# Attention scores in two 64-row halves of the matmul array, with a 0/1 mask factor after the exp, in a block-sparse attention and MLP kernel

## The chip, the cores and the metric

The kernel runs on one core of one Trainium2 chip. The metric is device time in microseconds of one execution; the median over three runs of the kernel before is 324.76 us (324.6 to 324.99).

## What is computed

Batch 4, 8 heads, 768 positions, head size 64. The mask is built from 24 blocks of 32 positions: neighbours, the first and the last block, and three sampled blocks for each block of queries.

```python
scores = (q @ k^T) / sqrt(64)                # for each batch and head, 768 x 768
scores = where(mask, scores, -1e9)
attn   = softmax(scores)
x      = (attn @ v), heads side by side      # 4 x 768 x 512

a1  = alpha1 * x + beta1
tok = w_tok @ a1                             # over the 768 positions
u   = x + lam * tok
a2  = alpha2 * u + beta2
out = u + lam * (relu(a2 @ w_ch1) @ w_ch2)   # 512 -> 2048 -> 512
```

## The kernel before

**Units.** Two heads of one batch make a pair; there are 16 pairs, four for each batch, pair i belonging to batch i // 4. A pair has 12 units (i, c, j): c is one of two halves of 384 queries, j says which head of the pair (j // 3) and which two of its six key tiles of 128 (j % 3). A step s of the main loop (L735) works on one unit and on what else is due then.

**A step's order on TensorE.** `emit_qk` (L310) makes the scores of the step's unit: two matmuls of 88 rows (L324), one for each key tile, with 384 query columns, into two banks of one `sp` tile. 64 of the rows are the head size; the other 24 carry the mask: rows 64 to 87 of `kTs` hold, for each key, a value of 0 or -400 for each block of queries, and the same rows of `qTs` hold which block a query is in. A masked score so becomes -400 lower, and the exp (L332, ScalarE) gives 0 for it. Then comes poured work: `pour` (L650 on) takes matmul jobs of the MLP from a queue by credit (L553 the first product, L572 the second, L485 the mixing of positions, `job_tok`). Last comes `emit_pv` (L337) for the unit of two steps ago (`LAG = 2`): six matmuls (L345) that take the exp's output `eT` as weights and `vext` (v with a column of ones) as 65 moving columns. `emit_finish` (L354) divides by the sum, and `emit_a1pp` (L369) makes a1, on GpSimd but for a batch's last half.

**How q and k get there.** `emit_load` (L105) loads q, k and v of a pair from HBM on GpSimd's queue, with a cast to 16 bits, into `qr`, `kr`, `vr` with two buffers each. For pairs 1 to 5, `emit_lay` (L116) copies q and k side by side into `qk` on VectorE, and `emit_tps` (L264) transposes on TensorE, 12 transposes of 128 x 128 for a pair, from where VectorE copies into `kTs` (L273) and `qTs` (L276). From pair 6 (`XP = 6`), `emit_lay` copies q and k into `ql` and `kl`, padded to 128 columns for each tile and with the mask's columns put there once (`emit_mask_cols`, L281, six transposes of 24 rows at L285; `emit_mask_spread`, L290, on GpSimd), and `emit_tdma` (L298) issues one DMA transpose for q and one for k on SP's queue, 12 tiles each, at the fourth and fifth step of the pair before.

**Order.** The schedule is written out by hand: `slots` (L667 to L725) says at which step each piece of the first batch is emitted; the engines take their instructions in the order of emission. PSUM has two `sp` tiles, three `mm` tiles (poured work, transposes, other small products) and one `op` tile; `eT` has five buffers. SP's queue carries the DMA transposes of q and k, those of `uraw` (`emit_udma`) and the output. After the last unit the rest of the MLP of the last batch runs alone.

Of the kernel before, what the change touches and what calls it, by code (L numbers as in the profile page):

```python
# [11 lines left out]
FP = mybir.dt.float32  # L12
F16 = mybir.dt.float16
BF = mybir.dt.bfloat16
I32 = mybir.dt.int32
AF = mybir.ActivationFunctionType
ALU = mybir.AluOpType
# [3 lines left out]
S = 768  # L21
D = 64
BLK = 32
NBLK = S // BLK
NR = 3
DM = 512
P = 128
NT = S // P
NH = 4 * DM // P
QC = 384  # L30
NP = H // 2
XP = 6
BIG8 = 400.0
SCALE = 1.0 / 8.0
EXPB = -0.35667494
# [6 lines left out]
def kernel(  # L42
# [16 lines left out]
    nc = tc.nc  # L59
# [3 lines left out]
    indq_np = (tok[None, :] // BLK == np.arange(NBLK)[:, None]).astype(  # L63
        ml_dtypes.bfloat16
    )
# [9 lines left out]
    ms_np = np.concatenate([mstat_np] + [kbi_np] * NR, axis=1)  # L75

    ident_dr = nc.inline_tensor(np.eye(P, dtype=ml_dtypes.bfloat16), name="ident_c")
    indt_np = np.ascontiguousarray(
        indq_np.reshape(NBLK, NT, P).transpose(2, 1, 0).reshape(P, NT * NBLK)
    )  # L80
    indt_dr = nc.inline_tensor(indt_np, name="indt_c")
    indq_dr = nc.inline_tensor(indq_np, name="indq_c")
    ident8_dr = nc.inline_tensor(np.eye(8, dtype=np.float32), name="ident8_c")
    ms_dr = nc.inline_tensor(ms_np, name="ms_c")
# [4 lines left out]
    ap_ = ctx.enter_context(tc.tile_pool(name="attn", bufs=1))  # L89
# [4 lines left out]
    def ptile(shape, dt, name):  # L94
        return pp.tile(shape, dt, name=name, tag=name)
# [6 lines left out]
    raws = {}  # L102
    qks = {}

    def emit_load(i, which="qkv"):  # L105
        b, hp = i // NP, i % NP
        for nm, src, dt in (("q", q, BF), ("k", k, BF), ("v", v, F16)):
            if nm not in which or (i, nm) in raws:
                continue
            t = ap_.tile([P, 2, NT * D], dt, name=nm + "r", tag=nm + "r", bufs=2)  # L110
            nc.gpsimd.dma_start(  # L111
                t[:], src[b, 2 * hp : 2 * hp + 2].rearrange("w (p o) d -> p w (o d)", o=NT)
            )
            raws[(i, nm)] = t

    def emit_lay(i, nm, w=slice(0, 2), copy=None):  # L116
        raw = raws[(i, nm)][:, w].rearrange("p w (o d) -> p w o d", d=D)
        if nm != "v" and i >= XP:
            dst = (qls if nm == "q" else kls)[i % 2][:, w, :, 0:D]
        elif nm == "v":  # L120
            dst = vexts[i % NVB][:, w, :, 0:D]
        else:
            if i not in qks:
                qks[i] = ap_.tile([P, 2, NT, 2, D], BF, name="qk", tag="qk", bufs=2)
            dst = qks[i][:, w, :, "qk".index(nm), :]
        (copy or nc.vector.tensor_copy)(out=dst, in_=raw)  # L126


    for nm in "qkv":
        raws[(0, nm)] = ap_.tile(  # L130
            [P, 2, NT * D], FP, name=nm + "f", tag="otf_" + nm, bufs=1
        )
    sampi = ptile([P, 2 * NR], I32, "sampi")
    ms = ptile([P, (1 + NR) * NBLK], FP, "ms")
    identb = ptile([P, P], BF, "identb")
    NQB = 4
    qTs = [ptile([P, 2, S], BF, f"qTs{i}") for i in range(NQB // 2)]
    kTs = [ptile([P, 2, S], BF, f"kTs{i}") for i in range(NQB // 2)]
    qText = [qTs[n // 2][:, n % 2] for n in range(NQB)]
    kText = [kTs[n // 2][:, n % 2] for n in range(NQB)]  # L140

    qls = [ptile([P, 2, NT, P], BF, f"ql{i}") for i in range(2)]
    kls = [ptile([P, 2, NT, P], BF, f"kl{i}") for i in range(2)]
    indt = ptile([P, NT, NBLK], BF, "indt")
    maskt = ptile([P, NT, NBLK], BF, "maskt")

    def load_first(nm, src, w, eng):
        eng.dma_start(
# [26 lines left out]
        )  # L175
    for i in range(2, NQB):
        nc.sync.dma_start(qText[i][D : D + NBLK, :], indq_dr.ap())
    nc.sync.dma_start(indt[:], indt_dr.ap().rearrange("p (o n) -> p o n", o=NT))
    warm = ptile([P, DM], BF, "warm")
    nc.vector.memset(warm[:], 0.0)  # L180
    for t in vexts:
        nc.gpsimd.memset(t[:, :, :, D : D + 1], 1.0)
    for t in qls + kls:
        nc.gpsimd.memset(t[:, :, :, D + NBLK : P], 0.0)

    gate = ptile([P, 1], FP, "gate")
    nc.gpsimd.tensor_copy(out=gate[:], in_=raws[(0, "v")][:, 0, 0:1])
# [60 lines left out]
    def mm_tile(shape=(P, DM), dt=FP):  # L248
        return psum.tile(list(shape), dt, name="mm", tag="mm", bufs=3)
# [28 lines left out]
            )  # L278
            qa = qb

    def emit_mask_cols():  # L281
        tps = mm_tile((P, NT, NBLK), BF)
        rows = slice(D, D + NBLK)
        for o in range(NT):
            nc.tensor.transpose(  # L285
                tps[:, o, :], kText[0][rows, ts(o, P)], identb[rows, rows]
            )
        nc.vector.tensor_copy(out=maskt[:], in_=tps[:])

    def emit_mask_spread():  # L290
        for ts_, src in ((qls, indt), (kls, maskt)):
            for t in ts_:
                nc.gpsimd.tensor_copy(
                    out=t[:, :, :, D : D + NBLK],
                    in_=src[:].unsqueeze(1).broadcast_to([P, 2, NT, NBLK]),
                )

    def emit_tdma(i, nm):  # L298
        dst, src = ((qTs, qls) if nm == "q" else (kTs, kls))
        nc.sync.dma_start_transpose(  # L300
            out=dst[i % 2][:].rearrange("p w (o t) -> p (w o) t", t=P),
            in_=src[i % 2][:].rearrange("p w o d -> p (w o d)"),
        )

    ets = {}
    ops = {}
# [3 lines left out]
    def emit_qk(i, c, j, spare=0):  # L310
        w, jp = j // 3, j % 3
        n = (2 * i + w) % NQB
        sp = sp_tile()
        for jj in range(2):
            for _ in range(spare if jj else 0):
                nc.tensor.matmul(
                    sp[:, 0, QC:],
                    warm[:, 0:P],
                    warm[:, 0:P],
                    start=False,  # L320
                    stop=True,
                    skip_group_check=True,
                )
            nc.tensor.matmul(  # L324
                sp[:, jj, 0:QC],
                kText[n][0 : D + NBLK, ts(2 * jp + jj, P)],
                qText[n][0 : D + NBLK, ts(c, QC)],
                start=True,
                stop=True,
            )  # L330
        eT = ap_.tile([P, 2, QC], F16, name="eT", tag="eT", bufs=5)
        nc.scalar.activation(  # L332
            eT[:], sp[:, :, 0:QC], AF.Exp, bias=expb[:], scale=SCALE
        )
        ets[(i, c, j)] = eT

    def emit_pv(i, c, j):  # L337
        w, jp = j // 3, j % 3
# [330 lines left out]
    def at(s, *fns):  # L669
        slots.setdefault(s, []).extend(fns)  # L670
# [15 lines left out]
    at(6, lambda: emit_bcast(0))  # L686
    at(7, lambda: emit_bcast(1))
    at(8, lambda: emit_bcast(2))
    at(13, emit_mask_cols)
    at(14, emit_columns_use)  # L690
    at(60, emit_lam16)
    at(57, emit_mask_spread)
    for i, where in {
        1: (5, 7, 11, 9, 12),
        2: (16, 17, 18, 21, 23),
        3: (20, 21, 28, 27, 32),
        4: (34, 35, 40, 37, 39),
        5: (41, 42, 45, 47, 51),
    }.items():
        for n, nm in enumerate("qkv"):  # L700
            at(where[n], lambda i=i, nm=nm: emit_lay(i, nm))
        for w in range(2):
            at(where[3 + w], lambda i=i, w=w: emit_tps(i, w))
    for i, nm, s in ((3, "qk", 9), (3, "v", 12), (4, "qkv", 22), (5, "qkv", 33)):
        at(s, lambda i=i, nm=nm: emit_load(i, nm))
    for o in range(NT):
# [25 lines left out]
        for fn in slots.get(s, ()):  # L732
            fn()

    for s in range(len(units) + LAG + 1):  # L735
        if s < len(units):
            i, c, j = units[s]
            r = s % 12
            emit_qk(i, c, j, zeros.get(s, 0))
            if r == 2 and i + 2 < NPAIR:  # L740
                emit_load(i + 2)
            if XP <= i + 1 < NPAIR:
                if r in (3, 4):
                    emit_lay(i + 1, "qk"[r - 3])
                    emit_tdma(i + 1, "qk"[r - 3])
                if r == 6:
                    emit_lay(i + 1, "v")
        if s >= OPEN:
            fns(s)
        if s in ready:  # L750
            i = ready.pop(s)
            tok, _ = pair_jobs(i)
            queue[0:2] = tok + [(0.0, lambda i=i: emit_udma(i))] + queue[0:2]
            scales[s + 7] = i
        if s in scales:
            emit_uscale(scales.pop(s))
        if s >= OPEN:
            pour()
        if LAG <= s < len(units) + LAG:


            i, c, j = units[s - LAG]
            if j == 1:
                emit_pv(i, c, 0)
            if j > 0:
                emit_pv(i, c, j)
            if j == NT - 1:
                emit_finish(i, c)
                last = (i % NP, c) == (NP - 1, 1)
                emit_a1pp(i, c, nc.vector if last else nc.gpsimd)  # L770
                if last:
                    phase["first"] = False
                    queue.extend(mlp_jobs(i // NP))
                    left = per_b if i >= NP else 2 * per_b - OPEN
                    state["rate"] = (sum(t[0] for t in queue) + 6.2 - CARRY) / left
                elif c == 1 and i >= NP:
                    ready[s + 5] = i
        if s < OPEN:
            fns(s)
# [33 lines left out]
```

## Time and profile before

| what | value | where |
|---|---|---|
| median of three runs | 324.76 us (324.6 to 324.99) | times |
| the profiled execution, first to last instruction | 323.1 us | page |
| first and last score matmul (L324) | 6.2 and 259.5 us | line L324 |
| mean granted TensorE clock | 1.000 | cores |
| L332 exp, ScalarE | 192 x 901 ns | part 5 |
| L324 scores, TensorE | 384 x 326 ns | part 5 |
| L553 and L572, TensorE | 512 x 325 ns, 368 x 379 ns | part 5 |
| L345, TensorE | 1152 with 65 columns, 193 ns each | part 5 |
| kl and ql copies, VectorE | 10 x 826 ns, 10 x 378 ns | part 5 by shape |
| L376 and L377, GpSimd | 28 x 1009 ns, 28 x 952 ns | part 5 |
| DMA transposes issued on SP (q, k, u) | 10, 10, 11 | part 6 by queue |

The span is the time from the first to the last instruction of the one profiled execution; no other time of that execution is recorded, and the median of the runs lies 1.66 us above it. A matmul's duration in the profile is a model with much overlap: two matmuls that start 0.163 us apart are both shown with 0.326. What TensorE spends on one is read from the starts. A row such as "24*128 24x24" gives the rows and columns of the array that a matmul uses, then the shape of what moves.

### The profile page before, as it was taken

Reading aid. Unit: us, or ns where it says so; the run is one execution under the profiler, and the core shown is the slowest. Engines: PE = TensorE matmul, PEld = TensorE weight load, DVE = VectorE, ACT = ScalarE, POOL = GpSimd, SP = SyncE. Lnnn points to the kernel's source line nnn. Section 1 sums busy time; section 2 is a strip of 40 time slices with the busy share of each in tenths; the row PEclk is TensorE's granted clock in tenths of the full one; section 3 lists DMA queues with packets and bytes.
Section 4 is the critical chain, followed back from the end, with each engine's and each line's share of the span. In section 5 each row is a group of like instructions: output and inputs, shape, how many; then the busy total and the mean of one; then the engine's idle time right before and its main releaser. Section 6 shows DMA issues by size and latency. Waiting matters only on the chain.

```text
span 323.1 us, 7663 instructions
## 1 busy us (share of the span) xinstructions
PE 315.6 (98%) x3216; PEld 205.7 (64%) x3216; DVE 140.0 (43%) x289; ACT 223.2 (69%) x328; POOL 99.0 (31%) x128
## 2 busy tenths in 40 slices
PE   8889999999999999999999999999999999999996
PEld 3667878667675766676665756676665756555543
DVE  4889988557343345331534444242332434000011
ACT  4889998998878776878768675678877740553310
POOL 7566746443434411132525402142222200000000
PEclk9999999999999999999999999999999999999999
DMA  6999996969392976091665966097430011000012
GB/s 168 197 191 164 143 156 110 165 114 140 57 177 54 169 120 131 32 172 27 127 103 96 138 106 128 34 155 74 108 52 32 15 46 65 32 34 32 32 43 89
DMA packets 61898, 32.56 MB, mean 101 GB/s; under 512 B 42000, under 2 KB 58756, under 8 KB 61736
## 3 DMA queue, kind: packets, MB, share of 16 engines
q0 software_dynamic: 16608, 14.22, 31.2%
q1 hardware_dynamic: 44680, 17.23, 25.2%
q10 hardware_dynamic: 576, 0.62, 0.7%
q8 instruction: 25, 0.41, 0.5%
q14 instruction: 9, 0.07, 0.1%
HBM read 29.97 MB, written 6.29 MB: 112 GB/s over the span
## 4 chain that ended last, share of the span: by engine, by line
PE 90%; DVE 7%; POOL 1%; issue 1%; ACT 1%; DVEq 0%; POOLq 0%
PE mm L553 26%; PE mm L572 25%; PE sp L324 16%; PE mm L485 10%; PE op L345 9%; PE op L260 1%; PE mm L592 1%; DVE qTs L276 1%; DVE wtokT L469 1%; DVE kTs L273 1%; PE mm L267 1%; DVE qk L126 1%; DVE x_sb L362 1%; POOL a1pp L376 1%; POOL a1pp L377 1%
## 5 line engine op out<-in xcount | busy, mean ns | idle before, releaser
L332 ACT ACTIVATE eT<-sp,expb 128x768 f16<-128x768 f32 x192 | 170.4, 901 | 47.3 <-PE sp L324 44.6
L553 PE MATMUL mm<-uT,w1b 128*128 128x384 bf16 x512 | 100.1, 325 | 0.0
L324 PE MATMUL sp<-qTs,kTs 88*128 88x384 bf16 x384 | 95.5, 326 | 0.9 <-ACT eT L332 0.5
L572 PE MATMUL mm<-w2b,hts 128*128 128x512 bf16 x368 | 92.3, 379 | 0.0
L560 ACT ACTIVATE hts<-mm 128x384 bf16<-128x384 f32 x128 | 61.8, 488 | 35.4 <-PE mm L553 35.0
L376 POOL TENSOR_TENSOR a1pp<-x_sb,vbc 128x384 bf16<-128x384 f32 x28 | 28.3, 1009 | 150.7 <-DVE x_sb L362 150.7
L553 PEld LDWEIGHTS <-w1b 128*128 128x128 bf16 x512 | 49.3, 97 | 36.1 <-issue 0.9
L345 PEld LDWEIGHTS <-eT 128*128 128x128 f16 x1152 | 55.9, 97 | 21.9
L572 PEld LDWEIGHTS <-hts 128*128 128x128 bf16 x368 | 35.3, 97 | 33.9
L345 PE MATMUL op<-vext,eT 128*128 128x65 f16 x1008 | 53.8, 193 | 0.0
L581 DVE TENSOR_TENSOR ot<-x_sb,mm 128x512 f32<-128x512 f32 x23 | 15.8, 686 | 66.9 <-PE mm L572 66.9
L485 PE MATMUL mm<-a1pp,wtokT 128*128 128x128 bf16 x576 | 41.6, 219 | 0.9 <-DVE qTs L276 0.3
L485 PEld LDWEIGHTS <-wtokT 128*128 128x128 bf16 x576 | 35.6, 97 | 6.6 <-PE mm L345 0.4
L500 DVE TENSOR_TENSOR x_sb<-x_sb,mm 128x384 f32<-128x384 f32 x32 | 17.6, 550 | 49.3 <-PE mm L485 48.5
L324 PEld LDWEIGHTS <-kTs 88*128 88x128 bf16 x384 | 28.3, 98 | 6.9 <-issue 1.4
L377 POOL TENSOR_TENSOR a1pp<-a1pp,vbc 128x384 bf16<-128x384 bf16 x28 | 26.7, 952 | 2.2
L506 DVE CAST ubf<-x_sb 128x384 bf16<-128x384 f32 x32 | 17.7, 553 | 1.1
L360 DVE RECIPROCAL rcp<-op 128x6 f32<-128x6 f32 x28 | 5.3, 191 | 29.5 <-PE op L345 29.2
L362 DVE TENSOR_TENSOR x_sb<-op,rcp 128x384 f32<-128x384 f32 x28 | 15.6, 558 | 1.0
L539 DVE TENSOR_SCALAR uT<-uraw,ab2T 128x768 bf16<-128x768 bf16 x11 | 5.4, 493 | 16.8 <-DMA uraw<-ubf 16.8
L111 POOL DMA_DIRECT2D qr<-in_q_dram x15 | 11.4, 761 | 3.1 <-DVE qk L126 3.1
L111 POOL DMA_DIRECT2D kr<-in_k_dram x15 | 10.8, 721 | 0.9 <-DVE qk L126 0.9
(74 smaller groups left out, 147.4 us busy)
## 6 DMA issues: line engine op xcount, KB each, us to landing
out_dram<-ot SPq DMA_DIRECT2D x23, 256.0 KB
qr<-in_q_dram POOLq DMA_DIRECT2D x15, 192.0 KB, 4.6
kr<-in_k_dram POOLq DMA_DIRECT2D x15, 192.0 KB, 6.3
vr<-in_v_dram POOLq DMA_DIRECT2D x15, 192.0 KB, 6.8
w1b<-in_moe_w_ch_dram POOLq DMA_DIRECT2D x4, 512.0 KB, 6.4
w2b<-in_moe_w_ch_dram POOLq DMA_DIRECT2D x4, 512.0 KB, 6.7
hts<-in_moe_w_tok_dram POOLq DMA_DIRECT2D x1, 1152.0 KB, 11.2
kf<-in_k_dram ACTq DMA_DIRECT2D x2, 192.0 KB
```

Of the source, the lines that this page charges most:

```text
L111: nc.gpsimd.dma_start(t[:], src[b, 2 * hp : 2 * hp + 2].rearrange("w (p o) d -> p w (o d)", o=NT))
L324: nc.tensor.matmul(sp[:, jj, 0:QC], kText[n][0 : D + NBLK, ts(2 * jp + jj, P)], qText[n][0 : D + NBLK, ts(c, QC)], start=True, stop=True,)
L332: nc.scalar.activation(eT[:], sp[:, :, 0:QC], AF.Exp, bias=expb[:], scale=SCALE)
L345: nc.tensor.matmul(op[:, w, o, :], eT[:, jj, ts(o, P)], vexts[i % NVB][:, w, 2 * jp + jj, :], start=(j == 0 and jj == 0 and o == 0), stop= ...
L362: nc.vector.tensor_tensor(out=x_sbs[b][:, ts(c, 3), cols].rearrange("p o (w d) -> p w o d", w=2), in0=op[:, :, :, 0:D], in1=rcp[:].unsquee ...
L376: eng.tensor_tensor(out=dst, in0=x_sbs[b][:, sl, cols], in1=bc[0], op=ALU.mult)
L377: eng.tensor_tensor(out=dst, in0=dst, in1=bc[1], op=ALU.add)
L485: nc.tensor.matmul(ps[:, o % 3, :], wtokT[:, os_, ts(o, P)], a1pps[i][:, os_, :], start=(os_ == 0 and o % 3 == 0), stop=(os_ == NT - 1 and ...
L506: nc.vector.tensor_copy(out=ubfs[i][:, sl, :], in_=x_sbs[b][:, sl, ts(hp, P)])
L553: nc.tensor.matmul(ps[:, 0:QC], w1b[:, dk, ts(n, P)], uTs[b][:, dk, ts(c, QC)], start=(dk == 0), stop=(dk == 3),)
L560: nc.scalar.activation(hts[(b, c)][:, n, :], ps[:, 0:QC], AF.Relu)
L572: nc.tensor.matmul(ps[:], ht[:, nk, ts(o % 3, P)], w2b[:, nk, :], start=(nk == 0), stop=(nk == NH - 1),)
```

## The change

For pairs 4 to 15 (batches 1 to 3, `MP = NP = 4`) the mask leaves the scores. The two score matmuls of a unit have 64 rows each, the first on array rows 0 to 63 and the second on rows 64 to 127, and VectorE multiplies the exp's output by a 0/1 mask of 768 x 768 in f16 that is made once (`emit_mask01`: 12 matmuls of 24 rows, in slots 19 to 49, and 12 comparisons). `emit_pv` of these pairs comes three steps after the scores instead of two, and `eT` gets a sixth buffer. Pairs 0 to 3 stay as they are.

The raw k tile, transposed in six tiles of 128 columns, has two key tiles side by side: rows 0 to 63 one, rows 64 to 127 the next (`khTs`). Queries must stand on both halves, so q is transposed twice, once as it is and once shifted by 64 columns, into every second tile of `qhTs`; it is loaded straight into a padded tile `qpads` for that. From pair 6 these are three DMA transposes on SP from the raw tiles, without VectorE copies; for pairs 4 and 5 they are 12 transposes on TensorE with four copies (`emit_tph`). `ql`, `kl`, `indt`, `maskt`, their memsets and the functions that filled them go; the first pair's f32 loads use a buffer of `x_sb`.

```diff
+MP = NP
+QS = 2 * NT + 1
...
+            if nm == "q":
+                t = qpads[i % 2][:, D : D + 2 * NT * D].rearrange(
+                    "p (w x) -> p w x", w=2
+                )
...
-        if nm != "v" and i >= XP:
-            dst = (qls if nm == "q" else kls)[i % 2][:, w, :, 0:D]
-        elif nm == "v":
+        if nm == "v":
             dst = vexts[i % NVB][:, w, :, 0:D]
...
-    qls = [ptile([P, 2, NT, P], BF, f"ql{i}") for i in range(2)]
-    kls = [ptile([P, 2, NT, P], BF, f"kl{i}") for i in range(2)]
-    indt = ptile([P, NT, NBLK], BF, "indt")
-    maskt = ptile([P, NT, NBLK], BF, "maskt")
+    qpads = [ptile([P, (QS + 1) * D], BF, f"qpad{i}") for i in range(2)]
+    qhTs = [ptile([P, QS, P], BF, f"qhT{i}") for i in range(2)]
+    khTs = [ptile([P, NT, P], BF, f"khT{i}") for i in range(2)]
+    mask01 = ptile([P, NT, S], F16, "mask01")
...
-    def emit_mask_cols():
...
-    def emit_mask_spread():
...
+    def emit_mask01(o, c):
         rows = slice(D, D + NBLK)
...
+        ps = mm_tile()
+        nc.tensor.matmul(
+            ps[:, 0:QC],
+            kText[0][rows, ts(o, P)],
+            qText[0][rows, ts(c, QC)],
+            start=True,
+            stop=True,
+        )
+        nc.vector.tensor_scalar(
+            out=mask01[:, o, ts(c, QC)],
+            in0=ps[:, 0:QC],
+            scalar1=-BIG8 / 2,
+            scalar2=None,
+            op0=ALU.is_ge,
+        )
+
+    def emit_tph(i, nm):
+        raw = raws[(i, nm)].rearrange("p w (m y) -> p (w m) y", y=P)
+        tps = mm_tile((P, NT, P), BF)
+        for m in range(NT):
+            nc.tensor.transpose(tps[:, m, :], raw[:, m], identb[:])
+        if nm == "k":
+            nc.vector.tensor_copy(out=khTs[i % 2][:], in_=tps[:])
+            return
+        dst = qhTs[i % 2]
+        nc.vector.tensor_copy(out=dst[:, 1 : QS - 1 : 2], in_=tps[:])
+        nc.vector.tensor_copy(out=dst[0:D, 2:QS:2], in_=tps[D:P])
+        nc.vector.tensor_copy(out=dst[D:P, 0 : QS - 1 : 2], in_=tps[0:D])
 
     def emit_tdma(i, nm):
-        dst, src = ((qTs, qls) if nm == "q" else (kTs, kls))
+        if nm == "k":
+            nc.sync.dma_start_transpose(
+                out=khTs[i % 2][:], in_=raws[(i, nm)].rearrange("p w x -> p (w x)")
+            )
+            return
+        dst, src = qhTs[i % 2], qpads[i % 2]
         nc.sync.dma_start_transpose(
-            out=dst[i % 2][:].rearrange("p w (o t) -> p (w o) t", t=P),
-            in_=src[i % 2][:].rearrange("p w o d -> p (w o d)"),
-        )
+            out=dst[:, 1 : QS - 1 : 2], in_=src[:, D : D + 2 * NT * D]
+        )
+        nc.sync.dma_start_transpose(out=dst[:, 0:QS:2], in_=src[:])
...
-        for jj in range(2):
+        for jj in range(2) if i >= MP else ():
+            rows = slice(D * jj, D * jj + D)
+            lo = NT * w + 3 * c + 1 - jj
+            nc.tensor.matmul(
+                sp[:, jj, 0:QC],
+                khTs[i % 2][rows, j],
+                qhTs[i % 2][rows, lo : lo + 3],
+                start=True,
+                stop=True,
+            )
+        for jj in range(2) if i < MP else ():
...
-        eT = ap_.tile([P, 2, QC], F16, name="eT", tag="eT", bufs=5)
+        eT = ap_.tile([P, 2, QC], F16, name="eT", tag="eT", bufs=6)
...
+    def emit_keep(i, c, j):
+        if i >= MP:
+            eT, jp = ets[(i, c, j)], j % 3
+            nc.vector.tensor_mul(
+                out=eT[:], in0=eT[:], in1=mask01[:, 2 * jp : 2 * jp + 2, ts(c, QC)]
+            )
...
-        4: (34, 35, 40, 37, 39),
-        5: (41, 42, 45, 47, 51),
...
+    for i, sv, sk, sq in ((4, 40, 37, 39), (5, 45, 47, 51)):
+        at(sv, lambda i=i: emit_lay(i, "v"))
+        at(sk, lambda i=i: emit_tph(i, "k"))
+        at(sq, lambda i=i: emit_tph(i, "q"))
+    for n, s in enumerate((19, 21, 23, 25, 27, 29, 31, 32, 37, 39, 48, 49)):
+        at(s, lambda n=n: emit_mask01(n // 2, n % 2))
...
+    pvs = {}
+    for u, (i, _, _) in enumerate(units):
+        pvs.setdefault(u + LAG + (i >= MP), []).append(u)
...
+            if s > 0:
+                emit_keep(*units[s - 1])
...
             if XP <= i + 1 < NPAIR:
                 if r in (3, 4):
-                    emit_lay(i + 1, "qk"[r - 3])
                     emit_tdma(i + 1, "qk"[r - 3])
...
-        if LAG <= s < len(units) + LAG:
...
-            i, c, j = units[s - LAG]
+        for u in pvs.get(s, ()):
+            i, c, j = units[u]
```

More of the change, by code (lines that the diff above doesn't have):

```diff
@@ L77 @@
     ident_dr = nc.inline_tensor(np.eye(P, dtype=ml_dtypes.bfloat16), name="ident_c")
-    indt_np = np.ascontiguousarray(
-        indq_np.reshape(NBLK, NT, P).transpose(2, 1, 0).reshape(P, NT * NBLK)
-    )
-    indt_dr = nc.inline_tensor(indt_np, name="indt_c")
     indq_dr = nc.inline_tensor(indq_np, name="indq_c")
@@ L109, in emit_load @@
                 continue
-            t = ap_.tile([P, 2, NT * D], dt, name=nm + "r", tag=nm + "r", bufs=2)
+            if nm == "q":
+                t = qpads[i % 2][:, D : D + 2 * NT * D].rearrange(
+                    "p (w x) -> p w x", w=2
+                )
+            else:
+                t = ap_.tile([P, 2, NT * D], dt, name=nm + "r", tag=nm + "r", bufs=2)[:]
             nc.gpsimd.dma_start(
-                t[:], src[b, 2 * hp : 2 * hp + 2].rearrange("w (p o) d -> p w (o d)", o=NT)
+                t, src[b, 2 * hp : 2 * hp + 2].rearrange("w (p o) d -> p w (o d)", o=NT)
             )
@@ L126, in emit_lay @@
         (copy or nc.vector.tensor_copy)(out=dst, in_=raw)
[L129 to L132, printed above, removed]
+    otf = ap_.tile([P, NT, DM], FP, name="x_sb", tag="x_sb", bufs=3)
+    for n, nm in enumerate("qkv"):
+        raws[(0, nm)] = otf[:].rearrange("p o d -> p (o d)")[
+            :, 2 * n * NT * D : 2 * (n + 1) * NT * D
+        ].rearrange("p (w x) -> p w x", w=2)
     sampi = ptile([P, 2 * NR], I32, "sampi")
@@ L177 @@
         nc.sync.dma_start(qText[i][D : D + NBLK, :], indq_dr.ap())
-    nc.sync.dma_start(indt[:], indt_dr.ap().rearrange("p (o n) -> p o n", o=NT))
     warm = ptile([P, DM], BF, "warm")
@@ L182 @@
         nc.gpsimd.memset(t[:, :, :, D : D + 1], 1.0)
-    for t in qls + kls:
-        nc.gpsimd.memset(t[:, :, :, D + NBLK : P], 0.0)
+    for t in qpads:
+        nc.gpsimd.memset(t[:, 0:D], 0.0)
+        nc.gpsimd.memset(t[:, QS * D :], 0.0)
     gate = ptile([P, 1], FP, "gate")
@@ L279, in emit_tps, with emit_tdma @@
             qa = qb
-    def emit_mask_cols():
-        tps = mm_tile((P, NT, NBLK), BF)
+    def emit_mask01(o, c):
         rows = slice(D, D + NBLK)
-        for o in range(NT):
-            nc.tensor.transpose(
-                tps[:, o, :], kText[0][rows, ts(o, P)], identb[rows, rows]
-            )
-        nc.vector.tensor_copy(out=maskt[:], in_=tps[:])
-    def emit_mask_spread():
[L291 to L298, printed above, removed]
-        dst, src = ((qTs, qls) if nm == "q" else (kTs, kls))
+        ps = mm_tile()
[25 more added lines that the diff above has]
+        nc.vector.tensor_copy(out=dst[D:P, 0 : QS - 1 : 2], in_=tps[0:D])
+    def emit_tdma(i, nm):
+        if nm == "k":
+            nc.sync.dma_start_transpose(
+                out=khTs[i % 2][:], in_=raws[(i, nm)].rearrange("p w x -> p (w x)")
+            )
+            return
+        dst, src = qhTs[i % 2], qpads[i % 2]
         nc.sync.dma_start_transpose(
-            out=dst[i % 2][:].rearrange("p w (o t) -> p (w o) t", t=P),
-            in_=src[i % 2][:].rearrange("p w o d -> p (w o d)"),
+            out=dst[:, 1 : QS - 1 : 2], in_=src[:, D : D + 2 * NT * D]
         )
+        nc.sync.dma_start_transpose(out=dst[:, 0:QS:2], in_=src[:])
     ets = {}
@@ L688 @@
     at(8, lambda: emit_bcast(2))
-    at(13, emit_mask_cols)
     at(14, emit_columns_use)
     at(60, emit_lam16)
-    at(57, emit_mask_spread)
     for i, where in {
@@ L733, in fns @@
             fn()
-    for s in range(len(units) + LAG + 1):
+    pvs = {}
+    for u, (i, _, _) in enumerate(units):
+        pvs.setdefault(u + LAG + (i >= MP), []).append(u)
+    for s in range(len(units) + LAG + 2):
+        if s == len(units):
+            emit_keep(*units[s - 1])
         if s < len(units):
@@ L739 @@
             emit_qk(i, c, j, zeros.get(s, 0))
+            if s > 0:
+                emit_keep(*units[s - 1])
             if r == 2 and i + 2 < NPAIR:
```

## The prediction

> **What bounds the kernel now.** I read the page's busy times first, then busy times by stretch, then the order of time around one step, and last the one place where the kernel already uses a part of the matmul array.
>
> The page, part 1 (engine, busy us, share, instructions):
>
> ```profile
> span 323.1 us, 7663 instructions
> ## 1 busy us (share of the span) xinstructions
> PE 315.6 (98%) x3216; PEld 205.7 (64%) x3216; DVE 140.0 (43%) x289; ACT 223.2 (69%) x328; POOL 99.0 (31%) x128
> ```
>
> PE leads, but matmuls overlap, so 98% is no proof. Busy time in the stretch that holds nearly all of pairs 5 to 15 (window, its length, then PE, PEld, DVE, ACT, POOL):
>
> ```profile
> 60.50:258.00 197.50, 197.50 (x2061) 129.66 (x2059) 78.87 (x152) 151.41 (x224) 62.89 (x74) 1.00 0.60 99
> ```
>
> PE never rests there; ACT works 77% of it, DVE 40%, POOL 32%, at a granted clock of 1.00. What one step costs is in the start times (start, duration, engine, line, shapes, count):
>
> ```profile
> 150.67 0.49 PE L324 MATMUL sp<-qTs,kTs 88*128 88x384 bf16 x2
> 151.00 0.81 PE L553 MATMUL mm<-uT,w1b 128*128 128x384 bf16 x4
> 151.65 0.35 PE L345 MATMUL op<-vext,eT 128*128 128x65 f16 x6
> 151.83 0.49 PE L324 MATMUL sp<-qTs,kTs 88*128 88x384 bf16 x2
> ```
>
> The reader is to take differences of starts, not durations: two score matmuls hold PE for 151.00 - 150.67 = 0.33 us, four L553 matmuls of the same 384 columns for 0.65 (0.163 each), six L345 matmuls for 0.18 (0.03 each). PE is fed without a gap: whatever is added to PE's stream after 60 us is added to the span, and whatever is taken away comes off until ACT or DVE fills up.
>
> **Part A, the scores of pairs 4 to 15.** 12 pairs x 12 steps = 144 steps. Before, a step has two matmuls of 88 rows one after the other, 0.33 us. After, the two use rows 0 to 63 and 64 to 127 and can stream side by side. If that is all, a step falls from 0.328 (2 x 0.163, and the first view's 0.33) to 0.163: 144 x 0.165 = **-23.8 us**. But between them run L345, L553, L572 and L485 with all 128 rows, so the array changes its division twice per step. The kernel does this once now, where six transposes of 24 rows (L285, rows 64 to 87) stand between 128-row work:
>
> ```profile
> 18.94 0.35 PE L345 MATMUL mm<-vext,eT 128*128 128x65 f16 x6
> 19.22 0.31 PE L285 MATMUL mm<-identb,kTs 24*128 24x24 bf16 x6
> 19.46 0.34 PE L324 MATMUL sp<-qTs,kTs 88*128 88x384 bf16 x1
> ```
>
> The same in narrower windows, where single ones are seen (last L345; L285 from the second on; last L285):
>
> ```profile
> 19.10 0.19 PE L345 MATMUL mm<-vext,eT 128*128 128x65 f16 x1
> ...
> 19.26 0.27 PE L285 MATMUL mm<-identb,kTs 24*128 24x24 bf16 x5
> ...
> 19.36 0.17 PE L285 MATMUL mm<-identb,kTs 24*128 24x24 bf16 x1
> ```
>
> The last L345 starts at 19.10 and is followed at 19.22: 0.12 instead of 0.03, so going in costs 0.09 to 0.10. The second L285 follows after 0.04. The last one starts at 19.36 and L324 at 19.46: 0.10 instead of the 0.025 that these transposes are otherwise apart, so coming out costs 0.075, or 0.09 counted from the end of its 24 columns. The one result that comes near, an exp that ends at about 19.2, is not read by L285 and is 0.26 earlier than L324. A step after is then 0.095 (in) + 0.04 (the second matmul behind the first) + 0.163 + 0.08 (out) = 0.378 us, against 0.328: +0.05 x 144 = **+7.2 us**. I take this, because a 24-row group between 128-row work is the nearest row there is to a 64-row pair between the same work. Its bounds: a free change -23.8; both changes paid and no overlap, 0.095 + 0.328 + 0.08 = 0.503, +25.2.
>
> The Trainium skill, TensorEngine Tiling (Array Packing), Key Properties, says that changing the tiling mode, not the tile, drains TensorE; it gives no time, and nothing there limits it to 24 rows. The Trainium skill, TensorE: Matmul & The Clock Gate, "Measured speedup vs the span model", lets a second tile start about 4 ns behind the first; by that the step would be 0.342 and part A +2.0 us. No run so far shows two tiles side by side.
>
> **Part B, the 0/1 mask.** Twelve matmuls of 24 rows by 384 columns, one in each of the slots 19 to 49, each alone between 128-row (or 88-row) work: 0.095 + 0.163 + 0.08 = 0.34 each, 4.1 us; out goes the L285 group, 19.46 - 19.10 - 0.03 = 0.33. In these slots (24.7 to 51 us) PE is not quite full: 12.17 of 12.60 us from 24.7 to 37.3 and 11.78 of 12.20 from there to 49.5. VectorE also gets 12 comparisons out of PSUM at about 0.55 (L500's 550 ns for 384 columns of f32), 6.6 us, eight of them in 24.7 to 37.3, where it is busy 11.31 of 12.60: 15.7 us of work. PE's addition there (8 x 0.34 = 2.7) and VectorE's overrun (3.1) are the same delay seen from two sides. Sum **+3.0**, bounds +1 (changes free, half in the gaps) and +5.
>
> **Part C, the factor on VectorE.** 144 products of 128x768 f16 in SBUF. The nearest rows (min/median/max ns):
>
> ```profile
> L453 DVE TENSOR_TENSOR w2b<-w2b,lam_bcb x4: 1204/1599/1939, 70.1 to 79.3; 128x2048 bf16<-128x2048 bf16 x4
> ...
> L126 DVE COPY kl<-kr x10: 347/1115/1160, 69.0 to 230.0; 128x768 bf16<-128x768 bf16 x10
> ```
>
> L453 alone takes 1204 for 2048 columns; less about 0.15 fixed that is 0.51 ns a column, so 768 cost 0.15 + 0.40 = 0.55 us. With POOL working beside it, L453 takes 1.94 and the copy 1.16 instead of 0.35, so 0.55 to 1.1 each. In 60.5 to 258 some 132 of them fall: 78.9 + 73 - 12.1 (the removed kl and ql copies, 8.3 + 3.8) = 140 us in about 204, covered by PE. If POOL's 32% delays a third of them by 0.5, 161. The cover is two steps of 1.1 to 1.5 us between a product and the L345 that reads it (the later slot for L345 and the sixth eT buffer pay for it), and it is gone in two places: 49.5 to 60.5, where VectorE has 9.64 us and gets 9 products and two comparisons (6.1, less 0.7 saved on pair 5's copies) in 11.0, 4.0 over, some 1.7 beyond the cover; and 70 to 80, 8.32 plus 4 less 1.5, 0.8 over. Queued behind a product that waits for its exp are the evacuations L500 and L581, and PE waits for those through the three mm buffers. **+2**, bounds 0 and +6.
>
> **At no cost.** Transposes by DMA: before, 2 issues a pair of 12 tiles each, after, 3 issues of 6, 6 and 7. They leave SP's queue at the same steps, wait for the load alone and not for a copy, and are needed some 8 steps (10 us) later; qTs and kTs issues take 1.4 and 2.1 us, so a third delays the output and uraw issues behind it by under 2 us. Exposed, it would be 1.4 x 10 = 14 us; that work of PE lies over it. Pairs 4 and 5 keep 12 transposes each on PE and save 0.7 us of VectorE each (four copies of 0.55 in place of four of 0.55 and two of 0.35). POOL loses 1.9 + 1.6 us of memsets and copies and gates nothing with them. The scratch moved into x_sb's buffer is free again 100 us before it is needed.
>
> **Sum.** +7.2 + 3.0 + 2.0 = +12.2 on the profiled 323.1 us: 335.3. The runs' median is 324.76, 1.66 above that span, which I keep: **337.0 us**. With each part at its nearer bounds (A +3 to +10): 329 to 346.
>
> **Rivals.** *The change of division is free* for 64-row tiles (the L285 gap being something of small transposes). For it: 88-row and 96-row matmuls stand beside 128-row ones without a gap. Against: both gaps have the same size and no waited-for event. Then -23.8 + 2 (12 x 0.163) + 2, and PE's stage of 197 falls to 176, of which ACT's 151 is 86%, so some 2 us come back: **307 us**. It decides from an in-and-out cost below 0.13 us a step. *VectorE becomes the bound*: each product meets POOL and takes 1.1, then 78.9 - 12.1 + 145 = 212 us against 197.5, +14.5 in place of A, +3 for B, +5 in the early stretch: **347**. For it: the copies at 1.1. Against: POOL is busy a third of the time. The Trainium skill, SBUF — State Buffer, "SBUF: two separate sides", states such a lock between a VectorE operation with two SBUF inputs and a GpSimd operation that reads SBUF; L453's 1.94 beside POOL agrees. *It doesn't do what it says*: the two matmuls stream one after the other: A +25.2, **355**.
>
> **How the numbers follow.** The forecast 0.55, the free change 0.22, VectorE bound 0.10, no overlap 0.10, cancelling to within 0.2% (what a measurement of this kernel can tell from no change) 0.03. Faster 0.23, same 0.03, slower 0.74. The range 309 to 352 leaves out about half of the free case and most of the serial one, 0.2 in all; the forecast's own is 329 to 346.
>
> **What would show it.** In the profile after: the start of the first score matmul 0.12 behind the last L345 and the next 128-row matmul 0.25 behind the second (right), or 0.03 and 0.16 (free); the two score matmuls 0.04 apart (right) or 0.163 (serial). The products near 0.55 to 0.7, VectorE under 80% after 60 us. PE gaps ended by VectorE beyond a few us would make part C the story. A stretch of a whole pair that is shorter than before makes the prediction wrong.

## The result, and the profile after

The changed kernel takes 341.47 us (median of four runs, 339.8 to 344.26) against 324.68 us: ratio 1.052, 95% interval 1.047 to 1.058. The forecast was 337.0 us, in a range of 309 to 352.

The lines of the changed kernel have other numbers than before: L338 makes the scores of 64 rows, L355 those of 88 rows, L286 the mask, L371 the product; L383, L523, L591 and L610 are what L345, L485, L553 and L572 were. Its page, part 1:

```profile
span 338.4 us, 7815 instructions
## 1 busy us (share of the span) xinstructions
PE 326.7 (97%) x3222; PEld 197.0 (58%) x3222; DVE 220.6 (65%) x420; ACT 224.7 (66%) x328; POOL 102.3 (30%) x124
```

Busy times in the same stretch as before (window, length, then PE, PEld, DVE, ACT, POOL):

```profile
60.50:258.00 197.50, 195.56 (x1990) 116.42 (x1989) 148.37 (x265) 147.65 (x216) 62.13 (x65) 1.00 0.60 94
```

VectorE has gone from 79 to 148 us there and still rests a quarter of the time. TensorE is nearly as full as before (195.56 of 197.50 us) and starts 1990 matmuls instead of 2061: it is busy for longer with less. Where that goes is in the order of time around two steps:

```profile
150.34 0.34 PE L338 MATMUL sp<-qhT,khT 64*128 64x384 bf16 x2
150.61 1.47 PE L591 MATMUL mm<-uT,w1b 128*128 128x384 bf16 x8
151.92 0.35 PE L383 MATMUL op<-vext,eT 128*128 128x65 f16 x6
152.20 0.34 PE L338 MATMUL sp<-qhT,khT 64*128 64x384 bf16 x2
152.47 0.82 PE L591 MATMUL mm<-uT,w1b 128*128 128x384 bf16 x4
```

Two score matmuls together show 0.34 us, hardly more than one alone (0.333 in part 5): they do run side by side. Over all 144 units the second starts 3 ns behind the first (median). But the six L383, which hold TensorE for 0.18 us elsewhere, are followed by the scores only after 152.20 - 151.92 = 0.28, and the scores by L591 after 0.27. Single starts give the medians: 0.126 us from the last L383 to the first score matmul instead of 0.029, and 0.265 from the second score matmul to the next one of 128 rows instead of 0.162. Going in costs 0.096 to 0.097, coming out 0.103. A step takes 0.096 + 0.003 + 0.265 = 0.364 us where it took 0.328.

A little more hides in the matmul that follows. The second of the two steps above in narrower windows (the last L383; the first L591; the second and third):

```profile
152.07 0.19 PE L383 MATMUL op<-vext,eT 128*128 128x65 f16 x1
...
152.47 0.34 PE L591 MATMUL mm<-uT,w1b 128*128 128x384 bf16 x1
...
152.64 0.49 PE L591 MATMUL mm<-uT,w1b 128*128 128x384 bf16 x2
```

The first L591 behind the scores holds TensorE for 152.64 - 152.47 = 0.17 us, the later ones for 0.16. By the medians of single starts it is 0.173 instead of 0.163, for L610 0.226 instead of 0.216, where the kernel before has 0.165 and 0.219 behind its 88-row scores. That is 0.008 more, so a step loses about 0.036 + 0.008 = 0.044 us.

The early part shows another loss. The order of time at 30 us, all engines (in brackets the idle time before an instruction, and what ended it; lines of other work left out):

```profile
30.14 0.50 PE L269 MATMUL mm<-identb,qk 128*128 128x128 bf16 x6
...
30.68 0.56 DVE L275 COPY kTs<-mm 64x768 bf16<-64x768 bf16 x1 [0.79 <-PE mm L269]
31.25 0.55 DVE L278 COPY qTs<-mm 64x768 bf16<-64x768 bf16 x1
...
31.86 0.33 PE L286 MATMUL mm<-qTs,kTs 24*128 24x384 bf16 x1 [1.22 <-DVE qTs L278]
32.12 0.11 PEld L355 LDWEIGHTS <-kTs 88*128 88x128 bf16 x2 [0.17 <-issue]
```

A mask matmul (L286) waits until VectorE has emptied the transposes of another pair, and the scores (L355) stand behind it in TensorE's order. The first score of pair 4 comes 5.0 us later than before, that of pair 5 8.9 us, that of pair 6 9.4, the last unit's 14.3, the end 15.3.

### The profile page after: what moved, and what is told of

It reads as the page before. It is cut to its first block, busy times and chain, and to the rows that moved or that the text cites. A ratio compares the mean times of both kernels' runs of the same rounds, so it can differ in the third digit from the quotient of the medians.

```text
span 338.4 us, 7815 instructions
## 1 busy us (share of the span) xinstructions
PE 326.7 (97%) x3222; PEld 197.0 (58%) x3222; DVE 220.6 (65%) x420; ACT 224.7 (66%) x328; POOL 102.3 (30%) x124
## 4 chain that ended last, share of the span: by engine, by line
PE 88%; DVE 8%; DMA 1%; ACT 1%; issue 1%; POOL 1%; DVEq 0%; POOLq 0%
PE mm L591 27%; PE mm L610 24%; PE sp L338 11%; PE mm L523 10%; PE op L383 9%; PE sp L355 3%; PE mm L630 1%; DMA x_sb<-in_q_dram 1%; DVE eT L371 1%; DVE qTs L278 1%; DVE kTs L275 1%; ACT eT L363 1%; PE mm L269 1%; PE mm L383 1%; DVE x_sb L400 1%
## 5 line engine op out<-in xcount | busy, mean ns | idle before, releaser
L371 DVE TENSOR_TENSOR eT<-eT,mask 128x768 f16<-128x768 f16 x144 | 97.2, 698 | 28.9 <-ACT eT L363 28.5
L591 PE MATMUL mm<-uT,w1b 128*128 128x384 bf16 x512 | 100.4, 327 | 0.9 <-DVE uT L577 0.9
L610 PE MATMUL mm<-w2b,hts 128*128 128x512 bf16 x368 | 92.5, 380 | 0.0
L414 POOL TENSOR_TENSOR a1pp<-x_sb,vbc 128x384 bf16<-128x384 f32 x28 | 32.4, 1157 | 162.4 <-DVE x_sb L400 146.9
L383 PEld LDWEIGHTS <-eT 128*128 128x128 f16 x1152 | 55.4, 97 | 23.1 <-DVE qTs L278 0.9
L591 PEld LDWEIGHTS <-w1b 128*128 128x128 bf16 x512 | 43.8, 97 | 39.4 <-issue 14.3
L383 PE MATMUL op<-vext,eT 128*128 128x65 f16 x1008 | 53.9, 193 | 0.1
L610 PEld LDWEIGHTS <-hts 128*128 128x128 bf16 x368 | 32.9, 98 | 35.1 <-issue 5.5
L338 PE MATMUL sp<-qhT,khT 64*128 64x384 bf16 x288 | 48.4, 333 | 0.0
L523 PE MATMUL mm<-a1pp,wtokT 128*128 128x128 bf16 x576 | 41.5, 220 | 0.8 <-DVE qTs L278 0.3
L523 PEld LDWEIGHTS <-wtokT 128*128 128x128 bf16 x576 | 32.8, 98 | 8.0 <-issue 5.3
L415 POOL TENSOR_TENSOR a1pp<-a1pp,vbc 128x384 bf16<-128x384 bf16 x28 | 28.7, 1027 | 2.2
L355 PE MATMUL sp<-qTs,kTs 88*128 88x384 bf16 x96 | 24.7, 327 | 1.7 <-ACT eT L363 1.3
L338 PEld LDWEIGHTS <-khT 64*128 64x128 bf16 x288 | 13.8, 92 | 15.0 <-issue 8.0
L114 POOL DMA_DIRECT2D qpad<-in_q_dram x15 | 11.4, 763 | 3.2 <-DVE qk L127 3.2
```

Source lines behind the costliest of these rows:

```text
L338: nc.tensor.matmul(sp[:, jj, 0:QC], khTs[i % 2][rows, j], qhTs[i % 2][rows, lo : lo + 3], start=True, stop=True,)
L355: nc.tensor.matmul(sp[:, jj, 0:QC], kText[n][0 : D + NBLK, ts(2 * jp + jj, P)], qText[n][0 : D + NBLK, ts(c, QC)], start=True, stop=True,)
L371: nc.vector.tensor_mul(out=eT[:], in0=eT[:], in1=mask01[:, 2 * jp : 2 * jp + 2, ts(c, QC)])
L383: nc.tensor.matmul(op[:, w, o, :], eT[:, jj, ts(o, P)], vexts[i % NVB][:, w, 2 * jp + jj, :], start=(j == 0 and jj == 0 and o == 0), stop= ...
L414: eng.tensor_tensor(out=dst, in0=x_sbs[b][:, sl, cols], in1=bc[0], op=ALU.mult)
L415: eng.tensor_tensor(out=dst, in0=dst, in1=bc[1], op=ALU.add)
```

## The experiments

All times are medians in us; before is 324.7 in each set, and the change 341.47.

| kernel | median | ratio to before, 95% interval |
|---|---|---|
| scores on all rows | 334.69 | 1.028 to 1.032 |
| both scores on one half | 362.81 | 1.113 to 1.119 |
| no product | 337.28 | 1.037 to 1.042 |
| two units together | 328.70 | 1.010 to 1.013 |
| mask by 88 rows | 340.50 | 1.046 to 1.051 |
| before, and the mask | 333.66 | 1.027 to 1.031 |
| before, and the mask's matmuls | 329.26 | 1.013 to 1.016 |
| before, and VectorE's part | 327.16 | 1.006 to 1.009 |
| from pair 6, one unit at a time | 333.21 | 1.025 to 1.028 |
| from pair 6, two units together | 321.30 | 0.988 to 0.991 |

**Scores on all rows.**

```diff
-            rows = slice(D * jj, D * jj + D)
-            lo = NT * w + 3 * c + 1 - jj
+            rows = slice(0, P)
+            lo = NT * w + 3 * c + 1 - (w and c)
```

> The changed kernel, but the two score matmuls of a unit past batch 0 use all 128 rows, so each sums two key tiles: the scores of pairs 4 to 15 are other numbers, and the array's division never changes between them and the rest. Theory (each change of division costs about 0.1 us, in and out, and this eats what side by side brings): a step goes from 0.364 us (0.125 after the last L345, 0.003, 0.265) back to 0.328 plus the usual 0.029, so 144 x 0.036 = 5.2 us less, about 335 to 336. Rival (side by side is worth its 144 x 0.16 = 23 us and VectorE's products eat it): some 15 to 23 us more, 355 or above.

334.69, as the theory had it. The order of time has the old pattern again:

```profile
150.50 0.49 PE L338 MATMUL sp<-qhT,khT 128*128 128x384 bf16 x2
150.83 0.81 PE L591 MATMUL mm<-uT,w1b 128*128 128x384 bf16 x4
151.48 0.35 PE L383 MATMUL op<-vext,eT 128*128 128x65 f16 x6
151.66 0.49 PE L338 MATMUL sp<-qhT,khT 128*128 128x384 bf16 x2
```

0.33 for the pair, 0.18 for six L383: two full matmuls one after the other are cheaper than two halves side by side with a change before and after.

**Both scores on one half.**

```diff
-            rows = slice(D * jj, D * jj + D)
-            lo = NT * w + 3 * c + 1 - jj
+            rows = slice(0, D)
+            lo = NT * w + 3 * c + 1
```

> The changed kernel, but both score matmuls of a unit past batch 0 use rows 0 to 63 (the second tile's scores are then those of the first's keys with other queries, so half of the scores of pairs 4 to 15 are not the reference's). The division changes as often as before, but the two can't stream side by side. Theory: the second starts 0.163 us behind the first instead of 0.003, 144 x 0.16 = 23 us more, about 363 to 365. Rival (the two did not overlap to any use, PE waits for VectorE instead): under 5 us more.

362.81, 21.3 more than the change, a little under the theory's 363.

```profile
150.72 0.49 PE L338 MATMUL sp<-qhT,khT 64*128 64x384 bf16 x2
151.15 0.82 PE L591 MATMUL mm<-uT,w1b 128*128 128x384 bf16 x4
```

0.43 from the first score to L591 instead of 0.27: the overlap is worth its 0.16 us a step. It is real, and it is spent. Set beside the kernel with the scores on all rows, this one also gives the price of the changes by itself: in both the two matmuls of a unit follow each other, and only here does the division change. The difference is 362.81 - 334.69 = 28.1 us, 0.195 a step.

**No product.**

```diff
     def emit_keep(i, c, j):
-        if i >= MP:
+        if False:
```

> The changed kernel without the product on VectorE, so that pairs 4 to 15 are not masked at all; the mask is still made. Theory (VectorE is covered after 66 us and costs only in pair 4's stretch, where the trace has PE gaps of 0.3 to 1.1 us ended by VectorE): 2 to 4 us less, 337 to 339. Rival (VectorE's products set the pace): 10 us less or more, under 331.

337.28. Three of its four runs kept the full clock and took 337.1 to 337.3; the change's two such runs 339.8 and 340.2. The product costs 2.5 to 3 us, and in the trace 2.1 of it lie between the first scores of pairs 4 and 5 (1.7 us lost there against 3.8). VectorE does not set the pace after that.

**Two units together.**

```diff
-    def emit_qk(i, c, j, spare=0):
+    def emit_sc(i, c, j, spare=0):
...
+        return sp
+
+    def emit_exp(i, c, j, sp):
...
-            emit_qk(i, c, j, zeros.get(s, 0))
+            if i < MP:
+                emit_exp(i, c, j, emit_sc(i, c, j, zeros.get(s, 0)))
+            elif s % 2 == 0:
+                two = [(u, emit_sc(*u)) for u in units[s : s + 2]]
+                for u, sp in two:
+                    emit_exp(*u, sp)
```

> The changed kernel with the scores of two units past batch 0 made together, at every second step, four 64-row matmuls in a row, then both exps: the array changes its division half as often, everything else the same. Theory: two units go from 2 x 0.364 to 0.125 - 0.029 + 0.003 + 0.163 + 0.003 + 0.265 = 0.53 us, 72 x 0.2 = 14 us less, about 327, less if TensorE must now wait for the second sp tile. Rival (VectorE's products set the pace): no change, 340 to 342.

328.70, 12.8 less, nearly the 14 of the theory. The edit changes how often the division changes, and with that it makes the scores of every second unit one step earlier; what the earlier scores do by themselves was not tested.

```profile
150.91 0.35 PE L386 MATMUL op<-vext,eT 128*128 128x65 f16 x6
151.19 0.50 PE L338 MATMUL sp<-qhT,khT 64*128 64x384 bf16 x4
151.62 1.18 PE L526 MATMUL mm<-a1pp,wtokT 128*128 128x128 bf16 x18
```

Four score matmuls (L386 and L526 are the lines that were L383 and L523) hold TensorE for 0.43 us, with 0.28 ahead of them as for two.

**Mask by 88 rows.**

```diff
     def emit_mask01(o, c):
-        rows = slice(D, D + NBLK)
+        rows = slice(0, D + NBLK)
```

> The changed kernel, but the twelve matmuls that make the mask take rows 0 to 87 instead of 64 to 87, which adds q times k (far below the 200 that the comparison needs) and leaves the array's division alone. Theory (each of the twelve pays a change in and out, about 0.2 us, in a stretch in which TensorE is nearly full): 12 x 0.2 = 2.4 us less, about 339, and fewer stretches at half clock near 30 us. Rival (the early loss is VectorE's twelve comparisons and the mm buffers they hold, not the changes): under 1 us less.

The theory failed here. 340.50 is within the spread of the change, and runs at the full clock are alike (339.6 and 339.8 against 339.8 and 340.2). Pair 4's first score comes 4.7 us late instead of 5.0. The changes are gone from the trace (a mask matmul that waits for nothing starts 0.03 us behind the last L383 instead of 0.125), and waits have taken their place: from step 19 to step 48 TensorE idles 3.7 us instead of 2.2, nearly all of it ended by VectorE's copies into `qTs`. In this kernel, then, a part of TensorE's added work and VectorE's delay do lie over each other. So it was split on the kernel before.

**Before, and the mask.**

```diff
+    mask01 = ptile([P, 2, S], F16, "mask01")
...
+    def emit_mask01(o, c):
...
+    for n, s in enumerate((19, 21, 23, 25, 27, 29, 31, 32, 37, 39, 48, 49)):
+        at(s, lambda n=n: emit_mask01(n // 2, n % 2))
```

> The kernel before with the twelve mask matmuls of 24 rows and the twelve comparisons at the changed kernel's slots, into a small tile that nothing reads. Theory (part B costs what pair 4's first score shows, 5.05 us later than before): 4 to 5.5 us above before, 329 to 330, part of it in stretches at half clock. Rival (TensorE's gaps there hide most of it): under 2 us.

333.66, 9.0 more (its four runs 7.9 to 10.0): worse than either expectation. The mask alone, so measured, is more than half of what the change loses. In the profiled execution 7.0 us are lost by pair 5's first score and 7.7 by the end. In the changed kernel 8.9 are lost by pair 5's first score, of which the products take 2.1 and the changes in pair 4's twelve steps up to 0.5, so 6.3 to 6.8 are left there for the mask.

**Before, and the mask's matmuls**, the comparison removed from that kernel:

```diff
-        nc.vector.tensor_scalar(
-            out=mask01[:, o % 2, ts(c, QC)],
...
-        )
```

> The kernel before with the twelve mask matmuls of 24 rows at the same slots and no comparison: nothing reads their result. Theory V (the mask with comparisons cost 8 to 9 us because VectorE, nearly full from 20 to 55 us, falls behind and holds the mm buffers): the matmuls alone cost little of it, 12 x 0.36 = 4.3 us at most and 1 to 3 after the gaps that TensorE has there, 326 to 328. Theory M (the matmuls with their changes of division are most of it): 330 or above.

**Before, and VectorE's part**, the matmul and its PSUM tile replaced:

```diff
+        two = warm[:, 0:QC].unsqueeze(1).broadcast_to([P, 2, QC])
+        nc.vector.tensor_tensor(out=mask01[:, :, ts(c, QC)], in0=two, in1=two, op=ALU.mult)
```

> The kernel before with twelve VectorE products of 128x768 (about 0.55 us, of a tile of zeros with itself) at the same slots, and no mask matmul and no PSUM tile. Theory V: VectorE's time alone brings most of the delay, 3 to 6 us, 328 to 331. Theory M: under 1 us, at most 326. If both this and the matmuls alone cost little, it is the mm buffer that a matmul's result holds until VectorE gets to it.

329.26 (4.6 more) and 327.16 (2.5 more). Neither theory alone: the matmuls cost their whole 12 x 0.36 us, VectorE's time adds 2.5, and together they cost 9.0, 2 more than the two apart (0.9 to 3.0 by the single runs of the kernel with both). The wait at 31.86 above is not these 2 us. It stands in the kernel with the matmuls alone too, as long and also ended by VectorE's copy into `qTs`, although there nothing reads what the mask matmul (L285 here) writes:

```profile
31.39 0.33 PE L285 MATMUL mm<-qTs,kTs 24*128 24x384 bf16 x1 [1.22 <-DVE qTs L277]
```

So a mask matmul waits for VectorE's copy of the transposes, not for a buffer that an earlier mask result holds; whether it waits for the copy's `mm` buffer or for the `qTs` that the copy writes and that it reads, no run tells. From 20 to 57 us the mask matmuls wait 1.8 us for such copies with the comparisons and 1.2 without, as VectorE comes to its copies later. That may be a part of the 2 us; where the rest arises stays open.

**From pair 6**, one unit at a time and two together, with the mask made by 88 rows in slots 58 to 69:

```diff
-MP = NP
+MP = 6
...
-        rows = slice(D, D + NBLK)
+        rows = slice(0, D + NBLK)
...
+        4: (34, 35, 40, 37, 39),
+        5: (41, 42, 45, 47, 51),
...
-    for n, s in enumerate((19, 21, 23, 25, 27, 29, 31, 32, 37, 39, 48, 49)):
+    for n, s in enumerate(range(58, 70)):
```

> As the kernel from pair 6 on, but one unit at a time, as in the change. Theory: 120 x 0.036 = +4.3, the mask +1.6, up to 2 us of gaps: 330 to 332; the early loss of the changed kernel (8.9 us at pair 5's first score) should be gone, under 1 us there. Rival (the early loss comes from the loads, the first buffers or other early parts, which stay): still 4 us or more at pair 5's first score and 336 or above.

> The scores of 64 rows from pair 6 on only, two units together, the mask by rows 0 to 87 made in slots 58 to 69, pairs 4 and 5 as before. Theory: 120 units x (0.53 / 2 - 0.328 = -0.063) = -7.5 us, the mask 12 x 0.163 - 0.33 = +1.6, up to 2 us of gaps: 319 to 322, faster than before. Rival (something else of the changed kernel, such as the product or the transposes, costs some microseconds everywhere): 325 or above.

One at a time takes 333.21, a little above the theory's 332. Pair 5's first score is 0.3 us earlier than before, not 8.9 later, so the early loss came with the mask, the first products or the new transposes of pairs 4 and 5, all of which are gone from there, and not with the loads and first buffers that stay. Pair 6's is 2.4 later, for the mask's 1.6 and some gaps, and the rest of the loss, 5.7 us by the end, comes with the steps (120 x 0.044 = 5.3). Two together takes 321.30, 1.1% less than before and the best of all kernels. Between these two kernels lie 11.9 us for 60 changes in and out, 0.2 each, as before. The page of the second:

```profile
span 319.6 us, 7760 instructions
## 1 busy us (share of the span) xinstructions
PE 308.3 (96%) x3190; PEld 191.1 (60%) x3222; DVE 208.7 (65%) x400; ACT 221.4 (69%) x328; POOL 101.6 (32%) x124
```

## Why the prediction was right, and where it was not

**The forecast's mechanism is what happened.** TensorE was the bound, the overlap would have brought 23.8 us, and the two changes of division took it back and more: shown by the two kernels that remove the one and the other, and by the one that halves the changes. The time itself came out 4.5 us above the forecast, because part B was far too small.

**Part A** was +0.05 a step, 7.2 us. By starts it is 0.364 - 0.328 = 0.036, 5.2 us, and with the 0.008 that the next matmul holds TensorE longer 0.044, 6.3 us; taking the changes out gained 6.3 to 6.7 (333.5, that kernel's run at nearly full clock, against 339.8 and 340.2). Of its terms, going in (0.095) measured 0.096; the second matmul's delay (0.04 from L285) is 0.003; coming out (0.08) is 0.103, and 0.11 with what the next matmul takes. So the sum came out nearly right because two errors of 0.03 to 0.04 and opposite sign cancelled, and that was luck. The 24-row transposes were the right row for the drain and the wrong one for two different tiles: of the 0.04 from the first L285 to the second, 0.025 is the distance of any two of them, and the other 0.015 looks like the 0.01 that the first matmul behind a change holds longer here. On that delay the Trainium skill, TensorE: Matmul & The Clock Gate, "Measured speedup vs the span model", has about 4 ns, and the trace agrees with its 3 ns. That a change of tiling mode drains TensorE, as the Trainium skill, TensorEngine Tiling (Array Packing), Key Properties, has it, agrees with the 0.096 and 0.103 us here.

**Part B is the term that was mis-sized**: +3.0, at most +5, and 9.0 measured on the kernel before, 6.3 to 6.8 by the trace of the changed kernel. Two steps failed. The gaps of TensorE in 20 to 55 us were taken to hide a part; the matmuls alone cost 4.6, so they hide none. And TensorE's addition and VectorE's overrun were called the same delay seen from two sides; on the kernel before they add, 4.6 and 2.5, and together cost 2 more than their sum. The mask by 88 rows shows that they are not wholly apart either, as there 2.4 us less of TensorE's work gained nothing. What the prediction did not have is that mask matmuls wait for VectorE's copies of another pair's transposes, 1.2 us at once at 31.86.

**Part C** was +2, and is 2.5 to 3, where it was put. The row for one product, minimum, median and maximum in ns:

```profile
L371 DVE TENSOR_TENSOR eT<-eT,mask x144: 543/557/1357, 57.7 to 275.1; 128x768 f16<-128x768 f16 x144
```

0.55 alone, as worked out (median of 90); the other 54 of the 144 had a GpSimd computation beside them, with a median of 0.89. The Trainium skill, SBUF — State Buffer, "SBUF: two separate sides", holds that such a product and a GpSimd operation that reads SBUF shut each other out; these two medians agree.

**The rivals.** The free change is ruled out by both gaps; no overlap by the 3 ns and by the one-half kernel; VectorE as the bound by the kernel without products, which should have gained 10 us and gained 2.5 to 3. That the transposes by DMA cost nothing was not tested by a run of its own; from pair 5 on the kernel with the scores on all rows, which has them too, runs at the pace of the kernel before (0.1 us lost in all).

## What to carry to other kernels

Two tiles of the array side by side pay only if enough of their matmuls stand together: here one pair saves 0.16 us and a change in and out costs 0.2 us, so group them until the overlap outweighs the change, and look in the old trace for any odd-sized matmul between full ones to get that price before writing anything. Gaps of an engine ahead of the steady part do not make work that is added there free; on two engines that wait for each other it cost more than the sum here. Put one-off work where its evacuating engine has room, as slots 58 to 69 did here.

## What was not expected of the hardware

In five of the profiled executions TensorE's granted clock is 0.50 for one stretch of 3.41 us, behind a stretch in which its matmuls were sparse though TensorE never idled for more than 1.3 us at a time. Two such windows of the kernel with two units together, the second at the lower clock (after the busy times: clock, DMA share, GB/s):

```profile
63.62:67.03 3.41, 1.32 (x15) 0.66 (x14) 3.38 (x8) 1.69 (x2) 0.00 (x0) 1.00 1.26 202
67.03:70.44 3.41, 3.41 (x18) 1.53 (x18) 1.67 (x4) 1.26 (x3) 0.00 (x0) 0.50 1.21 199
```

TensorE was busy 1.32 of 3.41 us while VectorE was full, and the next 3.41 us ran at half clock. The five stretches begin at 33 us (scores on all rows, no product) or at 66 to 67 us (both scores on one half, two units together, mask by 88 rows). Busy time alone does not decide it: with the scores on all rows 2.20 us of work from 29.98 to 33.40 were followed by a half-clock stretch, and less work, later in the same execution, was not:

```profile
64.11:67.52 3.41, 1.89 (x21) 1.02 (x19) 3.35 (x8) 2.44 (x3) 0.00 (x0) 1.00 1.28 200
67.52:70.93 3.41, 3.18 (x31) 2.09 (x31) 2.67 (x8) 2.31 (x5) 0.00 (x0) 1.00 1.25 206
```

Such stretches fit the spread of the change's runs: mean clocks of 1.000 and 0.999 with 339.8 and 340.17 us, 0.990 with 342.77, 0.985 with 344.26, the last two worth two and three such stretches (3.41 x 0.5 / 342 is 0.005 each). If that is what they are, the early waits cost once more, 0 to 4.5 us by chance, and 1.7 us of the median; where in those two runs the clock was low is not recorded. What keeps the clock was not tested.
